# Fourier mixing and a gated MLP on one core: the transform along D as seven products in the stream of the sequence transform, the result transposed, and the gate computed from padded columns of w1

## The chip, the cores and the metric

The kernel runs on one core of a Trainium2 chip. The metric is device time in microseconds (us): the median of three runs of the kernel before is 736.44 us (736.27 to 736.62). Times of single instructions come from one profiled execution.

## What is computed

The input `x` is one sequence of S = 2048 rows with D = 512 columns, in float32. Two branches are computed from it and mixed by a gate:

```python
g = sigmoid((x * gate_w).sum(-1, keepdims=True))       # one number for each row
a = x @ Wd_re.T;  b = x @ Wd_im.T                      # transform along D
A = Ws_re @ a - Ws_im @ b                              # transform along S, 2048 x 2048 matrices
B = (silu(x @ w1) * (x @ w3)) @ w2                     # F = 1376 inner columns
out = g * A + (1 - g) * B
```

The kernel takes the transform along S first, on `x`, and the one along D after it, which gives the same `A`.

## The kernel before, in words

**Numbers.** Every float32 operand of a product is split into a high part (ScalarE, `split`, line 77) and a low part (VectorE, line 78), and every product of two tiles is three products on TensorE (`mm3`, line 82): high by high, high by low, low by high. A product here means one instruction with a 128 x 128 stationary tile and 512 moving columns. A 2 x 2 block product is done with seven block products instead of eight, from sums of the blocks ("forms").

**Stages, in the order of TensorE.**

1. *Gate and up, first half* (`gate_up(1, NC)`): the 1376 columns of w1 and w3 are padded to 11 units of 128 (NC = 11). Unit `i` makes `silu(x w1) * (x w3)` for 1024 rows of x. Its weights are loaded (`load_w`), split into `wa{i}` (`prep_wa`, three units ahead) and, after four sums on VectorE (`wu{i}`), into `wb{i}` (`prep_wb`, one unit ahead). `first1` and `first2` make two of the seven products three units ahead; `second` makes the other five and the tile `h{i}`. VectorE adds results in PSUM (lines 184, 201, 203), ScalarE applies Silu.
2. *Down, first half* (`down(0, ...)`): 11 groups of 24 products accumulate h @ w2 for those rows in all eight PSUM banks. Group `c` needs the splits `ho{i}` and `w2o{i}` of unit i (`prep_dn`), made one group ahead in two buffers each. Between groups stand pieces of other work (`extra`): the loads and splits of x for the second half, and `load_score`, which multiplies x by `gate_w` and sums along a row. At the end the eight banks are copied out and stored to DRAM (`bsp`).
3. *Gate and up, second half* (units 11 to 21), and
4. *Down, second half* (`down(1, ...)`, units 11 to 21): here the extra pieces are `load_a(p)`, p = 0 to 7, which loads a piece `xr{p}` of x and makes the forms of x as the stationary operands `a1_p` and `a2_p`, and the first steps of the next stage.
5. *Sequence transform* (`fourier_step`, lines 503 to 549): four blocks of 7 forms (P1, P5, P6, P3, P7, P2, P4) x 4 steps of 12 products. The moving operands are the blocks of the transform matrices (`cc`), loaded on SP five steps ahead (`advance`), summed into forms on VectorE (`sum_c`, line 462), split three steps ahead into one of four `zo` buffers (`split_c`), and for T3 changed in place by an accumulating DMA from POOL's queue (line 473). Results are combined on ScalarE and VectorE and stored to DRAM as `zsp`.
6. *Transform along D* (`dft_hid`): 384 products read `zsp` back through `load_z`; each result tile of 128 rows is scaled by the gate, a number for each partition, and added to the scaled `bsp` tile (lines 606 and 608), then stored.

**What sets the order.** The tile framework orders the instructions of each engine when the program is built, and every engine runs its own list strictly in that order, SP's and POOL's DMA issues too. The 13 buffers `f4` (128 x 1024 float32) serve all loads, the `h` tiles and the staging; a load is issued when its buffer is free.

Of the kernel before, what the change touches and what calls it, by code (L numbers as in the profile page):

```python
# [28 lines left out]
def fnet_swiglu_gate_kernel(  # L29
# [3 lines left out]
    xs: bass.AP,  # L33
# [5 lines left out]
    gw: bass.AP,  # L39
    out: bass.AP,  # L40
):

# [42 lines left out]
    gw_sb = const.tile([P, D], F32, tag="gw", name="gw_sb")  # L85
    score = const.tile([P, NST], F32, tag="score", name="score")
    gate_t = const.tile([P, NST], F32, tag="gate_t", name="gate_t")
    ngate_t = const.tile([P, NST], F32, tag="ngate_t", name="ngate_t")
    bsp = dram.tile([S, D], F32, tag="bsp", name="bsp")
    zsp = dram.tile([4 * NTB * P, 1024], F32, tag="zsp", name="zsp")  # L90

# [87 lines left out]
    def first2(i):  # L179

        y = bank(4 + i % 2, f"Y{i}")
        prod(y, i, 1, 1, True)
        s1 = G[i][1]
        nc.vector.tensor_add(s1, s1, y)
        nc.scalar.activation(s1, s1, AF.Silu)

    def second(i, between):
# [18 lines left out]
        prod(x, i, 6, 2, False, True)  # L206
        nc.scalar.activation(g1, x, AF.Silu)
# [18 lines left out]
    def down(g, extra):  # L226
        e = g * NC + NC - 1
        late = [6 + (e + 1) % 2, 6 + e % 2, e % 4]
        order = [k for k in (4, 5, 0, 1, 2, 3) if k not in late] + late
        acc = [bank(k, f"acc{g}_{k}") for k in order]  # L230
        for c in range(NC):
            if c + 1 < NC:
                prep_dn(g * NC + c + 1)
            h, w = HO.pop(g * NC + c), W2O.pop(g * NC + c)
            for i in range(2 * NT):
                sl = slice(i * P, (i + 1) * P)
                mm3(acc[i], h[:, 0, sl], h[:, 1, sl], w[:, 0], w[:, 1], c == 0, c == NC - 1)
            if c in extra:
                extra[c]()
        for i in range(NT):  # L240
            o = wide(f"b{g}_{i}")
            nc.scalar.activation(o[:, :512], acc[2 * i], AF.Copy)
            nc.vector.tensor_copy(o[:, 512:], acc[2 * i + 1])
            r0 = (2 * g * NT + 2 * i) * P
            nc.sync.dma_start(bsp[r0 : r0 + 2 * P, :].rearrange("(a p) d -> p a d", a=2),
                              o.rearrange("p (a d) -> p a d", a=2))
        return order

    def gate_up(i0, i1):
        for i in range(i0, i1):  # L250
# [10 lines left out]
            def b1(i=i):  # L261
                if i + LOOK < i1:
                    first2(i + LOOK)

# [9 lines left out]
    nc.scalar.activation(score[:, :1], warm[:, :1], AF.Silu)  # L274
# [47 lines left out]
    nc.sync.dma_start(gw_sb, gw.to_broadcast([P, D]))  # L322
# [60 lines left out]
    def load_score(p):  # L383
        r, t = wide(f"sr{p}"), wide(f"st{p}")
        nc.sync.dma_start(r, xs[p])
        for j in range(2):
            u = 2 * p + j
            sl = slice(j * 512, (j + 1) * 512)
            nc.vector.scalar_tensor_tensor(t[:, sl], r[:, sl], 1.0, gw_sb, op0=ALU.mult,
                                           op1=ALU.mult, accum_out=score[:, u : u + 1])  # L390

# [3 lines left out]
    for p in range(NG):  # L395
        extra.setdefault(1 + p, []).append(lambda p=p: load_score(p))
# [15 lines left out]
    def flat(ap):  # L412
        return ap.rearrange("p a n -> p (a n)")

    def load_a(p):

        r = wide(f"xr{p}").rearrange("p (a n) -> p a n", a=4)
        m = wide(f"xm{p}").rearrange("p (a n) -> p a n", a=4)  # L420
        nc.sync.dma_start(flat(r), xn[p])
        a21, a11, a12, a22 = (r[:, i] for i in range(4))
        nc.vector.tensor_sub(m[:, 0], a22, a21)
        for d, v, w in ((1, m[:, 0], a11), (2, a12, m[:, 1])):
            nc.vector.scalar_tensor_tensor(m[:, d], v, -1.0, w, op0=ALU.mult, op1=ALU.subtract)
        nc.vector.tensor_sub(m[:, 3], a11, a21)
        split(A1[p][:, 0, 0], A1[p][:, 1, 0], a11)
        split(flat(A1[p][:, 0, 1:4]), flat(A1[p][:, 1, 1:4]), flat(m[:, 0:3]))
        split(flat(A2[p][:, 0, 0:2]), flat(A2[p][:, 1, 0:2]), flat(r[:, 2:4]))
        split(A2[p][:, 0, 2], A2[p][:, 1, 2], m[:, 3])  # L430
# [6 lines left out]
    NQ = NG // 2  # L437
    NJ = len(CHAIN) * NQ
    NSTEP = NTB * NJ
# [5 lines left out]
    LOADS = sorted((tb * NJ + n + q, tb, k, q)  # L445
                   for tb in range(NTB) for q in range(NQ)
                   for k, n in ((0, 0), (1, NQ - 1), (2, 2 * NQ - 1), (3, 5 * NQ)))

    def step_of(m):
        tb, r = divmod(m, NJ)  # L450
        j, q = divmod(r, NQ)
        return tb, q, *CHAIN[j]

    def sum_c(m):

        if not 0 <= m < NSTEP:
            return
        tb, q, k, form = step_of(m)
        b = {"T1": "B11", "T2": "B22", "T4": "B21"}.get(form)
        if b:  # L460
            t = RAW[tb, "B12", q]
            nc.vector.tensor_add(t, t, RAW[tb, b, q])  # L462

    def split_c(m):

        if not 0 <= m < NSTEP:
            return
        tb, q, k, form = step_of(m)
        src = RAW[tb, {"T1": "B12", "T2": "B12", "T4": "B12", "T3": "B22"}.get(form, form), q]
        t = ZO[m] = zo.tile([P, 2, 1024], F32R, tag="zo", name=f"zo{m}")  # L470
        split(t[:, 0], t[:, 1], src)
        if form == "B22":
            nc.gpsimd.dma_start(src, cc[tb, 1, q], accum_op=ALU.add)

    def advance(m):
        while LOADS and LOADS[0][0] <= m + LEAD + AHEAD:
            _, tb, k, q = LOADS.pop(0)
            r = RAW[tb, BLOCKS[k], q] = wide(f"c{k}_{tb}_{q}")
            nc.sync.dma_start(r, cc[tb, k, q])
# [4 lines left out]
    for p in range(NG):  # L484
        xacts[p].append(lambda p=p: load_a(p))
    xacts[7].append(lambda: advance(-4))
# [5 lines left out]
    nc.scalar.activation(gate_t, score, AF.Sigmoid)  # L492
    nc.vector.tensor_scalar(ngate_t, gate_t, -1.0, 1.0, op0=ALU.mult, op1=ALU.add)
    advance(-1)

    def spill(tb, k, t):
        nc.sync.dma_start(zsp[(tb * 4 + k) * P : (tb * 4 + k + 1) * P, :], flat(t))
# [5 lines left out]
    def fourier_step(m):  # L503
        tb, q, k, form = step_of(m)
        if q == 0 and k in ("P1", "P5", "P2"):
            banks = {"P1": XB[tb % 2], "P5": ZB, "P2": YB}[k]
            U[k] = [bank(b, f"{k}_{tb}_{r}") for r, b in enumerate(banks)]
        ps = U[{"P6": "P1", "P7": "P1", "P4": "P1", "P3": "P5"}.get(k, k)]
        z = ZO.pop(m)
        own = k in ("P1", "P5", "P2")  # L510
        for i in range(2):
            w = (A1 if k in ("P1", "P5", "P6", "P3") else A2)[2 * q + i]
            b = slice(i * 512, (i + 1) * 512)
            for r in range(2):
                sl = slice(r * P, (r + 1) * P)
                mm3(ps[r], w[:, 0, FORM[k], sl], w[:, 1, FORM[k], sl], z[:, 0, b], z[:, 1, b],
                    own and q == 0 and i == 0, q == NQ - 1 and i == 1, not own)
        advance(m)
        if q < NQ - 1:
            return  # L520

        def out(name):
            U[name] = ut.tile([P, 2, 512], F32, tag=name, name=f"z{name}_{tb}")
# [7 lines left out]
        if k == "P1":  # L531
            out("s1")
        elif k == "P5":
            out("p5")
        elif k == "P6":
            out("u2")
        elif k == "P3":
            plus("u2")
            spill(tb, 2, U["u2"])
        elif k == "P7":  # L540
            out("u3")
            nc.vector.tensor_add(flat(U["p5"]), flat(U["p5"]), flat(U["u3"]))
            spill(tb, 3, U["p5"])
        elif k == "P2":
            plus("s1")
            spill(tb, 0, U["s1"])
        else:
            out("c21")
            spill(tb, 1, U["c21"])


    DW, ZY = [], {}

    def load_d(q):
        r = wide(f"dr{q}")
        nc.sync.dma_start(r, dd[q])
        t = yd.tile([P, 2, 1024], F32R, tag=f"d{q}", name=f"d{q}")
        split(t[:, 0], t[:, 1], r)
        DW.append(t)

    def load_z(m):
        if m >= 4 * NTB:
            return
        r = wide(f"zr{m}")
        nc.sync.dma_start(r, zsp[m * P : (m + 1) * P, :])
        t = yz.tile([P, 2, 1024], F32R, tag="zy", name=f"zy{m}")
        split(t[:, 0], t[:, 1], r)
        ZY[m] = t

    N1 = NSTEP - 3 * NQ  # L570
    for n in range(N1):
        fourier_step(n)
    close(a1_cm)
    yd_cm, yd = pool("yd", 1, "left")
    yz_cm, yz = pool("yz", 4, "left")
    for n in range(N1, NSTEP):
        fourier_step(n)
        k = n - N1
        if k < 4:
            load_d(k)  # L580
        elif k < 8:
            load_z(k - 4)

    def cols(n):
        if n < NST - 1:
            return ((slice(0, D), nc.scalar),)
        return ((slice(0, D // 2), nc.scalar), (slice(D // 2, D), nc.sync))

    def dft_hid(tb):
        ks = (XB[0], ZB) if tb % 2 == 0 else (YB, XB[1])  # L590
        acc = [bank(k, f"y{tb}_{i}") for i, k in enumerate((*ks[0], *ks[1]))]
        for q in range(4):
            z, w = ZY.pop(tb * 4 + q), DW[q]
            for i in range(NT):
                for j in range(2):
                    sl = slice(j * 512 + i * P, j * 512 + (i + 1) * P)
                    b = slice(j * 512, (j + 1) * 512)
                    mm3(acc[i], z[:, 0, sl], z[:, 1, sl], w[:, 0, b], w[:, 1, b],
                        q == 0 and j == 0, q == 3 and j == 1)
            load_z(tb * 4 + q + 4)  # L600
        for i in range(NT):
            n = tb * NT + i
            t = ut.tile([P, 2, 512], F32, tag=("s1", "p5", "u2", "u3")[i], name=f"o{n}")
            b, o = t[:, 0], t[:, 1]
            nc.sync.dma_start(b, bsp[n * P : (n + 1) * P, :])
# [66 lines left out]
```

## Time and profile before

| | |
|---|---|
| median of the runs | 736.44 us |
| the profiled execution | 736.15 us, of which the span of instructions is 734.4 us |
| TensorE products / weight loads | 728.6 us busy, 3196 / 598.6 us |
| VectorE | 499.5 us busy, 645 instructions |
| ScalarE | 347.6 us busy, 455 instructions |
| GpSimd (POOL) | 14.3 us busy, 20 instructions |
| moved by DMA | 104.09 MB, mean 142 GB/s |

How to read it: the span is the time from the first to the last instruction of the profiled execution. A row of the chain of work is start, length and what. A row of the timeline is start, length, engine, line, operation, output<-inputs, shape, and in brackets the idle time before it with what ended it; neighbours of one kind are merged as "x2". A row of a group ends with the count, the busy time, the mean ns of one, the idle time before them and what ended it. A row of a DMA group has its count, its size and the median time from issue to landing. L82 is line 82 of the kernel.

### The profile page before, as it was taken

The numbers are of one execution on the slowest core, as the hardware profiler recorded it, in microseconds if no ns is written. First come the engines' busy times: TensorE is split into PE (matmuls) and PEld (weight loads), VectorE is DVE, ScalarE is ACT, GpSimd is POOL, SyncE is SP. The second block draws the span as 40 slices with busy tenths as digits, with TensorE's granted clock in tenths as the row PEclk, the third lists the DMA queues.
The fourth block names the chain that finished last, engine by engine and source line by source line (L and its number), as shares of the span: only waits on it lengthen the run. The fifth ranks groups of instructions, "written<-read, shape, count | busy, mean of one in ns | idle before, by whom it ended". The sixth has DMA issues, their size and how long they took to land.

```text
span 734.4 us, 8387 instructions
## 1 busy us (share of the span) xinstructions
PE 728.6 (99%) x3196; PEld 598.6 (82%) x3196; DVE 499.5 (68%) x645; ACT 347.6 (47%) x455; POOL 14.3 (2%) x20
## 2 busy tenths in 40 slices
PE   9999999999999999999999999999999999999997
PEld 5788888888888888888888888888888888888886
DVE  6997788793687768996857585758575858514331
ACT  6755553454554444763544454445444447323330
POOL 0000000000000000000010001000100010000000
PEclk9999999999999999999999999999999999999999
DMA  7112117533013002656297608770677159833331
GB/s 271 55 62 86 58 59 254 174 129 116 30 57 115 1 29 79 213 211 258 114 211 246 230 1 172 250 249 17 131 247 247 64 98 318 288 127 116 116 114 58
DMA packets 33464, 104.09 MB, mean 142 GB/s; under 512 B 3600, under 2 KB 3984, under 8 KB 33424
## 3 DMA queue, kind: packets, MB, share of 16 engines
q1 hardware_dynamic: 28816, 91.11, 35.4%
q0 software_dynamic: 2304, 8.39, 6.3%
q10 hardware_dynamic: 2304, 4.06, 1.5%
q8 instruction: 25, 0.41, 0.2%
q14 instruction: 15, 0.12, 0.1%
HBM read 86.77 MB, written 16.78 MB: 141 GB/s over the span
## 4 chain that ended last, share of the span: by engine, by line
PE 98%; DMA 1%; DVE 0%; SPq 0%; ACT 0%; DVEq 0%; issue 0%
PE P L82 41%; PE acc L82 16%; PE X L82 16%; PE y L82 12%; PE Z L82 8%; PE Y L82 4%; PE C L82 1%; DMA xs<-xt 1%; DVE xo L78 0%; ACT xo L77 0%; DVE o L608 0%; SPq L101 0%; DVEq L668 0%; SPq L132 0%; DVEq L608 0%
## 5 line engine op out<-in xcount | busy, mean ns | idle before, releaser
L82 PE MATMUL P<-zo,a 128*128 128x512 f32 x1344 | 304.9, 389 | 0.0
L82 PEld LDWEIGHTS P<-zo,a 128*128 128x128 f32 x1344 | 252.3, 188 | 52.4
L78 DVE TENSOR_TENSOR zo<-c,zo 128x1024 fp32r<-128x1024 f32 x112 | 137.1, 1225 | 80.5 <-ACT zo L77 79.8
L77 ACT ACTIVATE zo<-c 128x1024 fp32r<-128x1024 f32 x112 | 118.4, 1058 | 131.2 <-PE P L82 123.0
L82 PE MATMUL acc<-w2o,ho 128*128 128x512 f32 x528 | 120.1, 389 | 0.0
L82 PEld LDWEIGHTS acc<-w2o,ho 128*128 128x128 f32 x528 | 99.1, 188 | 20.7
L82 PE MATMUL X<-xo,wb 128*128 128x512 f32 x378 | 93.8, 390 | 0.0
L82 PE MATMUL y<-d,zy 128*128 128x512 f32 x384 | 87.2, 389 | 0.0
L82 PEld LDWEIGHTS y<-d,zy 128*128 128x128 f32 x384 | 72.1, 188 | 15.0
L82 PEld LDWEIGHTS X<-xo,wb 128*128 128x128 f32 x378 | 70.6, 188 | 15.6 <-DVE u L201 0.5
L462 DVE TENSOR_TENSOR c<-c,c 128x1024 f32<-128x1024 f32 x48 | 58.6, 1226 | 8.9 <-DMA c<-cc 7.7
L78 DVE TENSOR_TENSOR zy<-zr,zy 128x1024 fp32r<-128x1024 f32 x16 | 19.5, 1224 | 49.9 <-ACT zy L77 49.9
L77 ACT ACTIVATE zy<-zr 128x1024 fp32r<-128x1024 f32 x16 | 16.9, 1058 | 40.8 <-PE y L82 39.9
L77 ACT ACTIVATE wa<-ws 128x768 fp32r<-128x768 f32 (+2 forms) x23 | 18.8, 819 | 33.2 <-PE Z L82 32.0
L82 PE MATMUL X<-xo,wa 128*128 128x512 f32 x126 | 32.7, 391 | 0.0
L82 PE MATMUL Y<-xo,wa 128*128 128x512 f32 x126 | 32.5, 389 | 0.0
L82 PE MATMUL Z<-xo,wb 128*128 128x512 f32 x126 | 32.3, 389 | 0.0
L82 PE MATMUL Z<-xo,wa 128*128 128x512 f32 x126 | 32.2, 389 | 0.0
L78 DVE TENSOR_TENSOR wb<-wu,wb 128x1024 fp32r<-128x1024 f32 x21 | 25.7, 1225 | 8.2 <-ACT wb L77 8.1
L78 DVE TENSOR_TENSOR ho<-h,ho 128x1024 fp32r<-128x1024 f32 x22 | 27.0, 1225 | 2.4 <-ACT ho L77 2.4
L82 PEld LDWEIGHTS X<-xo,wa 128*128 128x128 f32 x126 | 23.4, 188 | 5.5 <-DVE wa L78 0.6
L82 PEld LDWEIGHTS Y<-xo,wa 128*128 128x128 f32 x126 | 23.7, 188 | 4.9
(78 smaller groups left out, 553.8 us busy)
## 6 DMA issues: line engine op xcount, KB each, us to landing
c<-cc SPq DMA_DIRECT2D x64, 512.0 KB, 4.6
ws<-w SPq DMA_DIRECT2D x21, 512.0 KB, 3.2
c<-cc POOLq DMA_DIRECT2D x16, 512.0 KB, 5.3
zr<-zsp SPq DMA_DIRECT2D x16, 512.0 KB, 5.6
w2r<-w SPq DMA_DIRECT2D x10, 512.0 KB, 3.5
xs<-xt SPq DMA_DIRECT2D x16, 256.0 KB, 5.1
sr<-xs SPq DMA_DIRECT2D x8, 512.0 KB, 4.1
bsp<-b SPq DMA_DIRECT2D x8, 512.0 KB, 3.0
```

Source lines behind the costliest of these rows:

```text
L77: nc.scalar.activation(hi, src, AF.Copy)
L78: nc.vector.tensor_sub(lo, src, hi.bitcast(F32))
L82: nc.tensor.matmul(ps, u, v, start=first and n == 0, stop=last and n == 2, skip_group_check=chain)
L462: nc.vector.tensor_add(t, t, RAW[tb, b, q])
```

## The change

- *The transform along D* joins the stream of the sequence transform as blocks 4 and 5 of 7 forms x 2 steps. The stationary operands are now the forms of D's matrices and the moving ones are blocks of `zsp`, so the result comes out transposed, D x S, and the kernel's output is transposed on the host. `dft_hid`, `load_d` and `load_z` leave.
- *D's forms* are made by `prep_d`, one piece in each of units 12 to 15, with `forms`, the code that `load_a` also uses. They lie in the two `ho` buffers until they are stored to DRAM (`dsp`), and are loaded as `D1` and `D2` during the last 12 steps of block 3.
- *The down stages* swap stationary and moving operand, so their results are transposed too. They are scaled by 1 - g at once, by a row tile `NG_T`, and stored as `nbsp`.
- *The gate* comes from the 32 padded columns of w1, which now hold `gate_w`: unit 10 (and 21) computes the score for each row of x on the way. `put_score` copies it out and stores it as `gs`; `gates(g)` loads it as a row for all 128 partitions, takes the sigmoid, makes 1 - g on VectorE, negates half of g and stores the tile (`gsp`), which is loaded again as `GT` before block 4. `load_score` and its loads leave.
- *The end*: in blocks 4 and 5 a result is multiplied by the gate on VectorE, `nbsp` is added to it by an accumulating DMA on POOL's queue, and SP stores it. The last result adds `nbsp` on VectorE instead.

```diff
+    def forms(r, m, t1, t2):
...
+        nc.vector.tensor_sub(m[:, 0], a22, a21)
+        for d, v, w in ((1, m[:, 0], a11), (2, a12, m[:, 1])):
+            nc.vector.scalar_tensor_tensor(m[:, d], v, -1.0, w, op0=ALU.mult, op1=ALU.subtract)
+        nc.vector.tensor_sub(m[:, 3], a11, a21)
+        split(t1[:, 0, 0], t1[:, 1, 0], a11)
+        split(flat(t1[:, 0, 1:4]), flat(t1[:, 1, 1:4]), flat(m[:, 0:3]))
+        split(flat(t2[:, 0, 0:2]), flat(t2[:, 1, 0:2]), flat(r[:, 2:4]))
+        split(t2[:, 0, 2], t2[:, 1, 2], m[:, 3])
+
+    def prep_d(p):
+        r, m = wide(f"dr{p}"), wide(f"dm{p}")
+        t1 = dn.tile([P, 2, 4, 256], F32R, tag="ho", name=f"d1_{p}")
+        t2 = dn.tile([P, 2, 4, 256], F32R, tag="ho", name=f"d2_{p}")[:, :, :3]
+        nc.sync.dma_start(r, dd[p])
+        forms(r, m, t1, t2)
+        nc.sync.dma_start(dsp[0][p], t1.bitcast(F32))
+        nc.sync.dma_start(dsp[1][p], t2.bitcast(F32))
...
+    def put_score(i, j, gate):
+        if i % NC < NC - 1:
+            return
+        if j == 0:
+            SC[i] = tp.tile([P, 2, 512], F32, tag="sc", name=f"sc{i}", bufs=1)
+        nc.scalar.activation(SC[i][F % P :, j], gate[F % P :], AF.Copy)
+        if j == 1:
+            nc.sync.dma_start(gs[2 * (i // NC) : 2 * (i // NC) + 2].rearrange("b o n -> o b n"),
+                              SC[i][F % P : F % P + 1])
...
             for i in range(2 * NT):
-                sl = slice(i * P, (i + 1) * P)
-                mm3(acc[i], h[:, 0, sl], h[:, 1, sl], w[:, 0], w[:, 1], c == 0, c == NC - 1)
+                sl = slice(i // 2 * P, (i // 2 + 1) * P)
+                b = slice(i % 2 * 512, (i % 2 + 1) * 512)
+                mm3(acc[i], w[:, 0, sl], w[:, 1, sl], h[:, 0, b], h[:, 1, b],
+                    c == 0, c == NC - 1)
...
             o = wide(f"b{g}_{i}")
-            nc.scalar.activation(o[:, :512], acc[2 * i], AF.Copy)
-            nc.vector.tensor_copy(o[:, 512:], acc[2 * i + 1])
...
+            nc.vector.tensor_mul(o[:, :512], acc[2 * i], NG_T[g][:, :512])
+            nc.scalar.activation(o[:, 512:], acc[2 * i + 1], AF.Copy)
+            nc.vector.tensor_mul(o[:, 512:], o[:, 512:], NG_T[g][:, 512:])
+            nc.sync.dma_start(nbsp[i * P : (i + 1) * P, g * 1024 : (g + 1) * 1024], o)
...
+    def gates(g):
+        t, NG_T[g] = wide(f"gt{g}"), wide(f"ng{g}")
+        nc.sync.dma_start(t.rearrange("p (b n) -> p b n", b=2),
+                          gs[2 * g : 2 * g + 2].rearrange("b o n -> o b n").to_broadcast([P, 2, 512]))
+        nc.scalar.activation(t, t, AF.Sigmoid)
+        nc.vector.tensor_scalar(NG_T[g], t, -1.0, 1.0, op0=ALU.mult, op1=ALU.add)
+        nc.scalar.activation(t[:, 512:], t[:, 512:], AF.Copy, scale=-1.0)
+        nc.sync.dma_start(gsp[g], t)
...
             def b1(i=i):
                 if i + LOOK < i1:
                     first2(i + LOOK)
+                if 0 < i - NC <= KD:
+                    prep_d(i - NC - 1)
...
-    for p in range(NG):
-        extra.setdefault(1 + p, []).append(lambda p=p: load_score(p))
+    extra.setdefault(2, []).append(lambda: gates(0))
...
+    NQ = [NG // 2] * NTB + [KD // 2] * (NTB // 2)
+    STEPS = [(blk, q, k, form) for blk, nq in enumerate(NQ) for k, form in CHAIN for q in range(nq)]
+    START = [sum(NQ[:blk]) * len(CHAIN) for blk in range(len(NQ) + 1)]
...
+    def block(blk, k, q):
+        if blk < NTB:
+            return cc[blk, k, q]
+        return z_rows(2 * (blk - NTB) + (0, 1, 1, 0)[k], (0, 0, 2, 2)[k] + q)
...
+    xacts[2].append(lambda: gates(1))
...
+    def spill(blk, k, t, ps=None):
+        last = blk == len(NQ) - 1 and k == 1
+        if blk < NTB:
...
+            return nc.sync.dma_start(z_rows(blk, k), flat(t))
...
+        for r in range(2):
+            nc.vector.tensor_mul(t[:, r], t[:, r] if ps is None else ps[r], gt)
+            if last:
+                nc.vector.tensor_add(t[:, r], t[:, r], b[:, r])
+                (nc.scalar if r else nc.sync).dma_start(o[:, r], t[:, r])
+        if not last:
+            nc.gpsimd.dma_start(t, nb, accum_op=ALU.add)
+            nc.sync.dma_start(o, t)
...
+    for n in range(N1, len(STEPS)):
+        k = n - N1
+        if k < 2 * KD:
+            nc.sync.dma_start((D1 + D2)[k].bitcast(F32), dsp[k // KD][k % KD])
+        elif k < 2 * KD + 2:
+            nc.sync.dma_start(GT[k - 2 * KD], gsp[k - 2 * KD])
+        step(n)
...
-    for tb in range(NTB):
-        dft_hid(tb)
...
+    w13[0, :, F:] = a["gate_w"][:, None]
```

212 lines of the change are left out of this document (77 added, 135 removed).

## The prediction

> **What bounds the kernel now.** I read the page's busy shares and its chain of work first, then the chain in order of time.
>
> ```profile
> span 734.4 us, 8387 instructions
> ...
> PE 728.6 (99%) x3196; PEld 598.6 (82%) x3196; DVE 499.5 (68%) x645; ACT 347.6 (47%) x455; POOL 14.3 (2%) x20
> ...
> PE 98%; DMA 1%; DVE 0%; SPq 0%; ACT 0%; DVEq 0%; issue 0%
> ```
> ```profile
> 113.95 59.88 PE acc L82 x264
> ...
> 278.72 59.88 PE acc L82 x264
> 338.60 304.69 PE P L82 x1344
> 643.29 87.05 PE y L82 x384
> 730.34 0.04 DVEq L608
> ```
>
> TensorE is the chain, and in the rows of the chain (start, length, what) each piece begins where the one before ends, up to 730.34 us: no gaps. So removed products are worth their full time, and everything else costs nothing until it makes TensorE wait. A product takes 87.05 / 384 = 0.2267 us. After the last one the span goes on for 734.4 - 730.34 = 4.06 us: the last arithmetic and the last store.
>
> ```profile
> 8.00:12.00 4.00, 4.00 (x19) 3.25 (x18) 3.62 (x7) 3.24 (x7) 0.00 (x0) 1.00 1.03 399
> ```
> ```profile
> 181.00:278.70 97.70, 97.70 (x432) 80.73 (x431) 68.15 (x104) 45.93 (x70) 0.00 (x0) 1.00 0.12 44
> 278.72:338.60 59.88, 59.88 (x265) 49.57 (x265) 55.63 (x95) 37.13 (x59) 0.00 (x0) 1.00 0.49 169
> 338.60:643.29 304.69, 304.69 (x1346) 252.26 (x1345) 206.88 (x181) 144.76 (x159) 14.06 (x16) 1.00 0.61 187
> ```
>
> These windows (columns PE, PEld, DVE, ACT, POOL, granted clock, DMA share, GB/s) give the cover. The clock is full, DMA reaches 399 GB/s where it is loaded. VectorE is the engine to watch: 55.63 of 59.88 us (93%) in the second down stage, 68.15 of 97.70 (70%) in the gate and up products before it, 68% in the sequence transform.
>
> **Products removed: -10.9 us.** The old D transform takes 384 products. The new blocks 4 and 5 take 2 blocks x 7 forms x 2 steps x 12 = 336. 48 x 0.2267 = 10.9 us. The down stages only swap the stationary and the moving operand, both 128 wide and 512 long as before; the count stays at 528.
>
> By the Trainium skill, "TensorE: Matmul & The Clock Gate", Back-to-back issue gap, products with 512 columns follow each other at about 131 ns; then 48 of them would be worth an estimated 6.3 us. The trace disagrees with 227 ns and decides.
>
> **VectorE's spacing.** A queue is walked with start-to-start times, which the timeline of a packed stretch gives:
>
> ```profile
> 302.67 1.23 DVE L78 TENSOR_TENSOR ho<-h,ho 128x1024 fp32r<-128x1024 f32 x1
> ...
> 319.00 1.24 DVE L78 TENSOR_TENSOR ho<-h,ho 128x1024 fp32r<-128x1024 f32 x1
> 320.13 0.97 DVE L78 TENSOR_TENSOR a<-xm,a 128x768 fp32r<-128x768 f32 x1
> 321.00 0.70 DVE L78 TENSOR_TENSOR a<-xr,a 128x512 fp32r<-128x512 f32 x1
> 321.61 0.44 DVE L78 TENSOR_TENSOR a<-xm,a 128x256 fp32r<-128x256 f32 x1
> 321.94 2.38 DVE L78 TENSOR_TENSOR zo<-c,zo 128x1024 fp32r<-128x1024 f32 x2
> ...
> 330.49 0.71 DVE L78 TENSOR_TENSOR w2o<-w2r,w2o 128x512 fp32r<-128x512 f32 x1
> ```
>
> 1024 columns take 1.13 us to the next start, 768 take 0.87, 512 take 0.61, 256 take 0.33. One preparation of a form tile (`forms`: four operations on 256, then splits of 256, 768, 512, 256) takes 5 x 0.33 + 0.87 + 0.61 + 0.33 = 3.46 us.
>
> **First down stage: 0.**
>
> ```profile
> 115.06 0.68 DVE L208 TENSOR_TENSOR h<-g,u 128x512 f32<-128x512 f32 x1
> ```
> ```profile
> L389 DVE SCALAR_TENSOR_TENSOR st<-sr,gw_sb 128x512 f32<-128x512 f32 x16 | 10.6, 689 | 2.2 <-DMA sr<-xs 2.2
> ```
>
> `load_score` leaves, 10.6 us of VectorE that lay under products, and `gates(0)` comes: a table load, a sigmoid, one VectorE operation. The row's load is issued when `wu13` is done, about 119.0 by the order after 115.06 (one split, four sums, two issues on SP). ScalarE then stops for it, and behind it wait `w2o3` and `ho3`. `ho3`'s low half is wanted at 113.95 + 3 x 5.44 + 0.2 = 130.5 us and ends 4.1 us after the load has landed (sigmoid 1.06, then 1.13 + 0.61 + 1.13 and signals), so the load may take 7.4 us. `put_score`'s two copies of 0.6 us delay only the last `h`, which is wanted nine groups later.
>
> **Gate and up, second half: +0.9 us.**
>
> ```profile
> L78 DVE TENSOR_TENSOR wb<-wu,wb 128x1024 fp32r<-128x1024 f32 x21 | 25.7, 1225 | 8.2 <-ACT wb L77 8.1
> ...
> L201 DVE TENSOR_TENSOR u<-u,X 128x512 f32<-128x512 f32 x21 | 14.4, 685 | 16.6 <-PE X L82 16.4
> ...
> L149 DVE TENSOR_TENSOR wu<-ws 128x256 f32<-128x256 f32 x21 | 8.9, 424 | 0.5
> ```
>
> `prep_d` puts one form preparation into each of four units. A unit lasts 42 products or 9.52 us and holds 0.87 + 1.13 + 4 x 0.33 + 5 x 0.61 = 6.4 us of VectorE by spacing; with 3.46 that is 9.8, 0.3 too much, 1.2 us in four units, which the lead of the splits takes up. Walking the printed order of the changed program, the four units still meet TensorE, but the splits `ho11` and `ho12`, which stand early now, have moved behind (D's tiles hold their buffers until stored), and the low half of `wb18` comes 0.9 us late. Bounds: 0, and 7.8 if every instruction held VectorE for its full duration (7.3 + 4.2 - 9.52 = 2.0, four times).
>
> **Second down stage: +3.0 us.** Here the cover is thin. In the printed order VectorE and ScalarE come to the gate row after `load_a(2)`. The row's load reuses the buffer of `xr1`, so it is issued at about 289.5; with 5.2 us or less it is there when ScalarE arrives.
>
> ```profile
> 290.74 2.40 SPq L421 DMA_DIRECT2D xr<-xn  x2
> ```
> ```profile
> 288.76 0.69 DVE L78 TENSOR_TENSOR a<-xr,a 128x512 fp32r<-128x512 f32 x1
> ```
> ```profile
> 293.49 1.19 ACT L77 ACTIVATE a<-xm 128x256 fp32r<-128x256 f32 x2 [1.34 <-DVE xm L426]
> ```
> ```profile
> L492 ACT ACT_TABLE_LOAD x1 | 1.3, 1283 | 0.0
> L77 ACT ACTIVATE zo<-c 128x1024 fp32r<-128x1024 f32 x112 | 118.4, 1058 | 131.2 <-PE P L82 123.0 <-issue 4.9 <-DMA c<-cc 1.7
> ```
> ```profile
> xr<-xn SPq DMA_DIRECT2D x8, 512.0 KB, 3.7
> ```
>
> ScalarE: 294.7 + 1.28 (table) + 1.06 (sigmoid) = 297.0; VectorE's complement (1.13) to 298.2; ScalarE's negated half (0.6) to 298.9. Only then does SP issue the store of the gate tile, and behind it in SP's queue stands the load of `xr3`, which today goes out at 290.74. It is issued at 299.6 and lands 3.7 later, with up to 1.3 more for the store's bytes ahead of it; I take 303.7. Until then VectorE does `ho15`, `w2o15`, `w2o16` and `ho16`, which ends at 303.4 (today 303.9, with `load_a(3)` already behind it). From 303.7 the order up to the last split of weights, `w2o21`, is 5 preparations (17.3), 5 `ho` (5.65), 5 `w2o` (3.05), 4 `zo` (4.5) and 2 sums (2.26): 32.8 us, so 336.5 plus 0.1 for the signal. TensorE wants `w2o21`'s low half at 338.60 - 24 x 0.2267 + 2 x 0.2267 = 333.6. It waits 3.0 us. Today `w2o21` ends at 331.2, so the 2.4 us of slack are what the first lateness eats. Bounds: 0, if the walk is late by its own error, and 8.6 with full durations (38.4 instead of 32.8 us).
>
> The scaled copies at the stage's end (8 VectorE operations for 4) free the first transform's banks first; I take 0.
>
> **The D stream's own waits: 0.** D's form tiles are written out (7 MB) and read back during the last 12 steps of block 3, 32.7 us; at 399 GB/s they need 18. In each new block VectorE has 20 operations on 1024 columns, 1 add of 1024 and 12 of 512: 31 us by spacing in 14 steps of 2.72, 38.1 us. The tightest wait is the accumulate that turns B22 into T3: two steps lie between the two, not four.
>
> ```profile
> c<-cc POOLq DMA_DIRECT2D x16, 512.0 KB, 5.3
> ...
> bsp<-b SPq DMA_DIRECT2D x8, 512.0 KB, 3.0
> ...
> zsp<-zu SPq DMA_DIRECT2D x4, 512.0 KB, 5.0
> ...
> gw_sb<-gw SPq DMA_DIRECT2D x1, 256.0 KB, 7.2
> ...
> out<-o SPq DMA_DIRECT2D x1, 128.0 KB, 1.7
> ```
>
> With 5.3 us block 5's T3 is ready about 1 us before it is wanted. Bounds 0 and 1. In SP's printed order every load of block 5 and the last load of `nbsp` stand ahead of the first output store, so stores that wait for an accumulate hold no load; behind the store of `zs1` of block 4 waits only a ScalarE read with a lead of three steps.
>
> **The tail: +3.2 us.**
>
> ```profile
> 731.33 0.34 SPq L610 DMA_DIRECT2D out<-o  x1
> ```
> ```profile
> DMA to landing us min/median/max: 5.1/5.3/6.7
> ```
>
> P2 of block 5 ends 2 steps, 5.44 us, before the end. VectorE adds and scales it in 4 x 0.61 plus 0.2, done 2.8 us before the end; the accumulate takes 5.3, SP issues the store 2.5 us after the end (0.33), it lands 3.0 later, and the last result's store goes beside it. Today the last store lands at 731.33 + 1.7 and the span ends 1.4 later; 2.5 + 0.3 + 3.0 + 1.4 = 7.2 against 4.06. Bounds: +0.9 (an accumulate as fast as a store, 3.0) and +6.6 (the slowest accumulate, 6.7, and a store of 5.0).
>
> By the Trainium skill, "DMA: Bandwidth & Descriptors", Anatomy of one DMA, a GpSimd DMA takes about 2.0 us and its bytes at 436 GB/s, an estimated 3.2 us for 512 KB; the tail would be 2.1 us shorter and the sum -5.9. The sixteen accumulates of the trace took 5.3.
>
> **Sum.** -10.9 + 0.9 + 3.0 + 3.2 = -3.8 us. The profiled execution took 736.15 us (span 734.4); the median of the runs is 736.44, 0.3 more. Forecast 736.15 - 3.8 = 732.4 us.
>
> **Rivals.**
> 1. *The cover holds.* VectorE's two lags stay inside the slack. For it: 2.4 us of slack now, and no TensorE wait today. Against: a fixed order that is 5 us later. 736.15 - 10.9 + 3.2 = 728.5.
> 2. *VectorE becomes the bound at full durations.* Each operation starts only when the one before has ended, as where it needs its result. 7.8 in gate and up, 8.6 in the second down stage: 736.15 - 10.9 + 7.8 + 8.6 + 3.2 = 744.9. It decides from a surplus of 10.9 - 3.2 = 7.7 us in both. Against it: the spacings above.
>  The Trainium skill, "VectorE: DVE Perf Modes", The DRAIN you can't avoid, says that the next operation does not start until the pipeline is empty, and speaks for this rival; the starts at 319.00 and 320.13 under a duration of 1.24 speak against it here.
> 3. *The gate row's broadcast load is the wait.* 128 partitions read one row. `gw_sb`, half as large, took 7.2 us; twice that, 14.4, exceeds the cover by 7.0 in the first and 9.2 in the second down stage: 732.4 + 16.2 = 748.6, and slower than before from 8.3 us on. Against: `gw_sb` stood in a queue that moved 399 GB/s, at the end of it.
>
> That the products stay is excluded: the printed program has 336.
>
> **How the numbers follow.** Forecast 0.45 (its own range 730 to 735), rival 1 0.25, rival 2 0.21, rival 3 0.09. A measurement of this kernel tells 0.2%, 1.5 us, from no change. Faster: 0.40 + 0.25 = 0.65; within: 0.05 of the forecast and 0.03 of rival 2, 0.08; slower 0.27. The range 728 to 740 leaves out rival 3, the upper part of rival 2 and a little below.
>
> **What would show it.** Blocks 4 and 5 as 336 products of 0.227 us; a TensorE wait of about 3 us for `w2o` near 334 us and about 1 us for `wb` before; `xr3` landing near 304; the span ending about 7 us after the last product, with an output store as the last landing. No wait at `w2o`, or one before `ho3` or `ho15`, makes the forecast wrong.

## The result and the profile after

| | before | after |
|---|---|---|
| median of the runs | 736.36 us (4 runs, 736.08 to 736.62) | 745.25 us (4 runs, 745.09 to 745.51) |
| ratio | | 1.0121, 95% interval 1.0104 to 1.0139 |
| profiled execution, its span | 736.15, 734.4 us | 745.09, 743.2 us |

The forecast was 732.4 us, with 728 to 740: the change costs 8.9 us where 4 were to be won. The page of the changed kernel, its busy shares and its chain of work:

```profile
span 743.2 us, 8371 instructions
...
PE 719.9 (97%) x3148; PEld 588.8 (79%) x3148; DVE 537.3 (72%) x685; ACT 368.8 (50%) x487; POOL 26.2 (4%) x31
...
PE 78%; issue 9%; DVE 6%; DMA 3%; ACT 1%; POOL 1%; SPq 0%; POOLq 0%; DVEq 0%; ACTq 0%
```

TensorE has 48 products less and is busy 8.7 us less, but it is 78% of the chain and not 98%. The timeline of TensorE (start, length, line, output<-inputs, number, and the wait before) has the stretches one after the other:

```profile
279.59 56.18 PE L81 MATMUL acc<-ho,w2o 128*128 128x512 f32 x245
337.48 4.61 PE L81 MATMUL acc<-ho,w2o 128*128 128x512 f32 x19 [1.70 <-DVE w2o L77]
341.92 304.81 PE L81 MATMUL P<-zo,a 128*128 128x512 f32 x1344
646.57 49.12 PE L81 MATMUL P<-zo,d 128*128 128x512 f32 x216
698.59 11.17 PE L81 MATMUL P<-zo,d 128*128 128x512 f32 x48 [2.89 <-ACT zs L589]
710.95 0.50 PE L81 MATMUL P<-zo,d 128*128 128x512 f32 x1 [1.19 <-ACT zu L589]
711.73 16.43 PE L81 MATMUL P<-zo,d 128*128 128x512 f32 x71 [0.27 <-DVE zo L77]
```

The sequence transform is as long as before. Block 4 (the first 168 of the `zo,d` products) runs through. Block 5 stops TensorE three times, for 4.4 us in all. The last product ends at 711.73 + 16.43 = 728.16, and the span goes on for 15.0 us after it, the tail. The timeline of POOL shows what it does in that time (L558 is the addition of `nbsp`, L510 the one that makes T3):

```profile
674.66 1.22 POOL L558 DMA_DIRECT2D zu<-nbsp  x1 [12.94 <-DVE zu L553]
681.18 1.21 POOL L558 DMA_DIRECT2D zp<-nbsp  x1 [5.29 <-DVE zo L77]
688.30 1.21 POOL L558 DMA_DIRECT2D zs<-nbsp  x1 [5.91 <-DVE c L499]
695.29 1.21 POOL L558 DMA_DIRECT2D zc<-nbsp  x1 [5.78 <-issue]
703.94 0.91 POOL L510 DMA_DIRECT2D c<-zsp  x1 [7.45 <-DVE zo L77]
705.17 0.87 POOL L510 DMA_DIRECT2D c<-zsp  x1 [0.33 <-issue]
718.09 1.20 POOL L558 DMA_DIRECT2D zu<-nbsp  x1 [12.05 <-DVE zu L553]
724.56 1.22 POOL L558 DMA_DIRECT2D zp<-nbsp  x1 [5.27 <-DVE zs L593]
731.84 1.20 POOL L558 DMA_DIRECT2D zs<-nbsp  x1 [6.06 <-issue]
```

Two additions of `nbsp` never stand closer than 6.5 us, whatever their data do, while the two T3 accumulates at 703.94 and 705.17 follow each other at once. "issue" as the releaser says that POOL waited for nothing that the profile shows. By the lines of L558, an addition takes this long from issue to landing:

```profile
DMA to landing us min/median/max: 6.2/6.8/7.0
```

And the waits of the last 97 us (who waited for whom, us in total, times, longest):

```profile
DVE zo L77 <- ACT zo L76: 23.5, 8, 7.3
ACT zo L76 <- DMA c<-zsp: 13.9, 4, 6.5
ACT zs L589 <- DMA out<-zs: 8.9, 1, 8.9
...
PE P L81 <- ACT zs L589: 2.9, 1, 2.9
```

ScalarE stops four times for T3 and once, for 8.9 us, before it may read block 5's P1 into the tile `zs`, since block 4's result in that tile is still to be stored. All these stops hold up the splits behind them.

### The profile page after: what moved, and what is told of

It is laid out like the page before. It is cut to its first block, busy times and chain, and to the rows that moved or that the text cites. A ratio compares the mean times of both kernels' runs of the same rounds, so it can differ in the third digit from the quotient of the medians.

```text
span 743.2 us, 8371 instructions
## 1 busy us (share of the span) xinstructions
PE 719.9 (97%) x3148; PEld 588.8 (79%) x3148; DVE 537.3 (72%) x685; ACT 368.8 (50%) x487; POOL 26.2 (4%) x31
## 3 DMA queue, kind: packets, MB, share of 16 engines
q0 software_dynamic: 4784, 14.16, 10.9%
## 4 chain that ended last, share of the span: by engine, by line
PE 78%; issue 9%; DVE 6%; DMA 3%; ACT 1%; POOL 1%; SPq 0%; POOLq 0%; DVEq 0%; ACTq 0%
PE P L81 38%; PE X L81 15%; PE acc L81 12%; PE Z L81 8%; PE Y L81 4%; DMA c<-zsp 3%; DVE a L77 1%; PE C L81 1%; DVE zo L77 1%; DMA xs<-xt 1%; DVE xm L102 0%; DVE ho L77 0%; DVE w2o L77 0%; DVE c L499 0%; SPq L625 0%
## 5 line engine op out<-in xcount | busy, mean ns | idle before, releaser
L77 DVE TENSOR_TENSOR zo<-c,zo 128x1024 fp32r<-128x1024 f32 x140 | 170.7, 1223 | 111.8 <-ACT zo L76 111.3
L76 ACT ACTIVATE zo<-c 128x1024 fp32r<-128x1024 f32 x140 | 147.4, 1059 | 168.8 <-PE P L81 136.8
L81 PE MATMUL acc<-ho,w2o 128*128 128x512 f32 x528 | 120.7, 390 | 1.8 <-DVE w2o L77 1.7
L81 PEld LDWEIGHTS acc<-ho,w2o 128*128 128x128 f32 x528 | 98.9, 188 | 23.3 <-DVE w2o L77 2.7
L81 PE MATMUL P<-zo,d 128*128 128x512 f32 x336 | 77.2, 390 | 4.4 <-ACT zs L589 2.9
L499 DVE TENSOR_TENSOR c<-c,c 128x1024 f32<-128x1024 f32 x60 | 73.2, 1223 | 8.1 <-DMA c<-cc 5.9
L81 PEld LDWEIGHTS P<-zo,d 128*128 128x128 f32 x336 | 62.9, 188 | 18.5 <-ACT zs L589 3.3
L510 POOL DMA_DIRECT2D c<-cc x16 | 14.0, 876 | 592.9 <-DVE zo L77 592.9
L81 PEld LDWEIGHTS Z<-xo,wb 128*128 128x128 f32 x126 | 23.7, 188 | 5.0
```

The source lines that it names most:

```text
L76: nc.scalar.activation(hi, src, AF.Copy)
L77: nc.vector.tensor_sub(lo, src, hi.bitcast(F32))
L81: nc.tensor.matmul(ps, u, v, start=first and n == 0, stop=last and n == 2, skip_group_check=chain)
L499: nc.vector.tensor_add(t, t, RAW[blk, b, q])
L510: nc.gpsimd.dma_start(src, block(blk, 1, q), accum_op=ALU.add)
```

## The experiments

Theory **Q**: the additions of `nbsp` are let in one at a time on GpSimd's queue, about 7 us apart; that makes block 4's store of `zs` late and with it ScalarE and TensorE, and it makes the tail long. Rivals: **B**, the single `zs` buffer alone; **L**, the 7 MB of form tiles read back at block 4's start; **W**, formed after the first runs, the stop for T3, which in these short blocks stands only two steps behind B22; **V**, no room on VectorE. Ratios are against the kernel before, with their 95% intervals; the changed kernel has 1.0121.

### 1 to 4: the additions, the buffer, the rows, the descriptors

```diff
 # e1_vector_add: as the last result has it, for all eight
+            nc.vector.tensor_add(t[:, r], t[:, r], b[:, r])     # b: loaded by SP at P1 and P3 of the block
-            nc.gpsimd.dma_start(t, nb, accum_op=ALU.add)
 # e2_two_zs
-            U[name] = ut.tile([P, 2, 512], F32, tag=name, name=f"z{name}_{blk}")
+            U[name] = ut.tile([P, 2, 512], F32, tag=name, name=f"z{name}_{blk}", bufs=2 if name == "s1" else 1)
 # e3_rows_4k
-    nbsp = dram.tile([D, S], F32, tag="nbsp", name="nbsp")
+    nbsp = dram.tile([NTB, 2, P, 2, 512], F32, tag="nbsp", name="nbsp")
 # e4_ring_2k
-    nc = bacc.Bacc("TRN2", target_bir_lowering=False, num_devices=1, dynamic_dma_scratch_size=1024)
+    nc = bacc.Bacc("TRN2", target_bir_lowering=False, num_devices=1, dynamic_dma_scratch_size=2048)
```

> All eight results of blocks 4 and 5 get their nbsp part as the last one does: a load by SP, some steps ahead, and two VectorE additions; GpSimd accumulates only the four T3 tiles. Theory Q (the nbsp accumulates admit each other only about 7 us apart on GpSimd's queue, so the store of zs of block 4 is late, the next block's read of P1 into that tile waits 8.9 us, and the tail is long): the TensorE waits of 2.9 and 1.2 us in block 5 go, the products end near 342.1 + 304.5 + 76.2 = 722.8, the span about 5.9 us later as the last result's own additions and store took in the changed kernel; span 728.7, time 730.6. Rival L (the 7 MB of form tiles read back delay block 4's and 5's own loads): the TensorE waits stay, products end at 728.2, time about 736. Rival V (VectorE has no room for sixteen more additions of 0.61 us): waits for zo in both blocks, time 733 or more.

> The tile zs of the blocks' first result gets a second buffer; everything else as in the changed kernel, the accumulates too. Theory Q: ScalarE's read in block 5 no longer waits 8.9 us and TensorE's 2.9 us go, but the accumulates still stand 7 us apart; T3 of block 5 may have to wait for zc of block 4 (3.5 us of TensorE) or not; the last store of zs lands at 733 to 736; time 735.5 to 739. Rival B (the single buffer is the whole cause, the queue's spacing costs nothing by itself): products end at 722.8, zs is done at 719.8 and its accumulate starts at once, 6.8 + 2.8 + 1.4 later the span ends; time near 732.5. Rival L (loads of the form tiles): no change, 745.

> The scratch nbsp is laid out so that each accumulate reads one run of 4 KB per partition (128 rows) in place of two of 2 KB (256 rows); the same bytes, the same queue, the same tiles. Theory Q with its cause in the number of rows (two accumulates of 128 rows were admitted 1.2 us apart at 703.94 and 705.17, never two of 256): the issues of block 4 follow the data (zp near 679.7, zs near 683.3), each lands about 5.3 us after its issue, no TensorE wait in block 5, time near 732. Rival S (GpSimd's accumulates are always one after the other, whatever their rows): issues 5.6 us apart, zs of block 4 issued near 685.9; time near 734. Rival L: no change, 745.

> Only the scratch memory for GpSimd's DMA descriptors is doubled, from 1024 to 2048 bytes per partition; the program is the same. Theory Q with its cause in room for descriptors: two accumulates of 256 rows stand in the queue at once, issues follow the data, each still lands about 6.8 us after its issue; zs of block 4 is stored by 693.5, TensorE does not wait in block 5, products end at 722.8, zs of block 5 lands near 726.6, time near 733. Rival S (one accumulate after the other for another reason): issues stay 6.5 to 7.1 us apart, time 745.

| | median us | ratio |
|---|---|---|
| e1_vector_add | 737.82 | 1.0016 (1.0007 to 1.0026) |
| e2_two_zs | 744.49 | 1.0114 (1.0095 to 1.0133) |
| e3_rows_4k | 739.60 | 1.0038 (1.0023 to 1.0053) |
| e4_ring_2k | 740.29 | 1.0053 (1.0037 to 1.0070) |

**The queue.** With twice the descriptor memory, and nothing else changed, POOL's additions of block 4 follow VectorE's results:

```profile
674.85 1.20 POOL L558 DMA_DIRECT2D zu<-nbsp  x1 [13.17 <-DVE zu L553]
680.47 1.20 POOL L558 DMA_DIRECT2D zp<-nbsp  x1 [4.42 <-DVE zp L553]
684.13 1.21 POOL L558 DMA_DIRECT2D zs<-nbsp  x1 [2.46 <-DVE zs L553]
687.37 1.21 POOL L558 DMA_DIRECT2D zc<-nbsp  x1 [2.04 <-DVE zc L553]
```

With half the rows for each DMA and the old memory it is the same:

```profile
681.71 0.87 POOL L559 DMA_DIRECT2D zp<-nbsp  x1 [4.64 <-DVE zp L554]
685.46 0.86 POOL L559 DMA_DIRECT2D zs<-nbsp  x1 [2.88 <-PE P L81]
688.72 0.86 POOL L559 DMA_DIRECT2D zc<-nbsp  x1 [2.39 <-DVE zc L554]
```

So what holds a DMA back is room for descriptors, counted in rows; rival S (additions always one after the other) is out. The Trainium skill, "DMA: Bandwidth & Descriptors", SWDGE vs HWDGE vs iDMA, says that GpSimd writes its descriptors into rings that lie in SBUF, and that only one queue is allocated to it. That a full ring holds up whatever comes next is read from these two runs.

**But neither run reached its 732 to 733.** Products still end at 728.7 and 727.6, since ScalarE still waits for the store of `zs`, here in e4:

```profile
ACT zs L589 <- DMA out<-zs: 7.9, 1, 7.9
```

Two or three additions now share the DMA engines with the stores. `zs` is issued at 684.13 and not at 688.30, its store on SP at 690.68 and not at 695.00, but ScalarE's read starts at 697.24 and not at 697.94: from the issue of the store to the read it was 2.9 us, and now it is 6.6, with the addition of `zc` under way beside it (that overlap is read from the times; it was not tried apart). What went is tail: 10.5 us instead of 15.0 (e4). Q has the tail right and is not the only cause of the stops.

**The buffer.** In e2 the stop for `zs` is gone, the products end 1.5 us sooner (726.7), and the rest stays. Both B (732.5) and Q (735.5 to 739) are wrong about its time. POOL shows what is next:

```profile
696.57 1.21 POOL L558 DMA_DIRECT2D zc<-nbsp  x1 [6.11 <-DVE c L499]
697.31 1.41 POOL L510 DMA_DIRECT2D c<-zsp  x1
704.00 0.87 POOL L510 DMA_DIRECT2D c<-zsp  x1 [5.28 <-issue]
```

T3 of block 5 comes in behind `zc`, its second half only when `zc` has landed; ScalarE waits for it, VectorE 8.4 us for ScalarE, and `zu`, whose work stands behind T3's split on both engines, is added at 716.89 against 718.09.

**VectorE additions.** e1 has no addition on POOL at all and still loses, in block 4 and 5:

```profile
DVE zo L77 <- ACT zo L76: 17.6, 9, 6.9
ACT zo L76 <- DMA c<-zsp: 12.3, 4, 7.3
...
PEld P L81 <- DVE zo L77: 5.9, 6, 1.6
```

ScalarE stops 7.3 us for T3, VectorE behind it 6.9 us. With 36 us of work in the 38 us of a block VectorE can't make that up. Q's 730.6 is out. V's "733 or more" holds, but V has no reason for the stop ahead of it. L's marks are nearly met: it set the end of the products at 728.2 and the time at about 736, and they came to 728.4 and 737.8; e6 decides on L. The stop for T3 is W, and the next runs try it.

### 5 to 8: no addition, another order, straight into out, the early stages

```diff
 # e5_no_nbsp
-            nc.gpsimd.dma_start(t, nb, accum_op=ALU.add)
 # e6_p2_before_p7: P2 between P3 and P7, in blocks 4 and 5 only
+    LATE7 = tuple(CHAIN[n] for n in (0, 1, 2, 3, 5, 4, 6))
 # e7_into_out: down() stores o into out, and
-            nc.gpsimd.dma_start(t, nb, accum_op=ALU.add)
-            nc.sync.dma_start(o, t)
+            nc.gpsimd.dma_start(o, t, accum_op=ALU.add)
 # e8_early_stages
-        nc.sync.dma_start(gsp[g], t)
+        nc.scalar.dma_start(gsp[g], t)
-        nc.scalar.activation(SC[i][F % P :, j], gate[F % P :], AF.Copy)      # put_score
+        nc.scalar.activation(o[:n], gate[:n], AF.Silu)                       # n = 96; the row is stored from o
```

> Leaves out the addition of nbsp to seven of the eight results of blocks 4 and 5: no accumulate stands between the scaling and the store. Theory A (the accumulates are the whole loss: their spacing, their traffic and the stores behind them): no TensorE wait in blocks 4 and 5, products end near 722.8, the span 5.9 later; time 730.6. Theory W (T3 stands only two steps behind B22 here, so ScalarE and then VectorE stop about 7 us for its accumulate in each block, and VectorE, which has 31 us of work in 38, comes late with the splits): TensorE waits of 1 to 3 us for zo near P7 of block 5 stay, products end at 724 to 726, time 732 to 734.

> In blocks 4 and 5 the products run P1, P5, P6, P3, P2, P7, P4: two more steps between B22 and T3. The accumulates of nbsp stay as they are. Theory W: ScalarE's waits for T3 (6.5 us in each block of the changed kernel) fall below 2, VectorE's idle 4 to 7 us before them go, and no TensorE wait is left in block 5; products end near 722.8. Then the accumulates, 7 us apart, set the end: zu lands at 716, zs at 723, zp at 730, its store 4.2 before the end; time 736.4. Theory A alone: T3 of block 5 still stands in GpSimd's queue behind zc of block 4 until 702, TensorE waits 2 us or more, products end at 725 or later, time 739 or more.

> The down stages store their part straight into out, and seven of the eight results of blocks 4 and 5 are accumulated into out by one GpSimd DMA from their tile; the load into the tile and the store behind it go. Same rows of 2 KB, so by theory Q the accumulates stay about 7 us apart; a tile is free 3 us sooner, TensorE's 2.9 us in block 5 shrink to 0 to 1, and the store of 2.8 us behind the last accumulate goes: time 739 to 740. Rival H (adding in the chip's memory costs more than adding in the tile, as the destination must be read there): 9 us or more for each, time 745 or more.

> Two edits before the sequence transform: the gate tile is stored from ScalarE's queue, so that SP's load of xr3 does not stand behind it, and the score row is stored from the tile it is in (Silu takes only the 96 partitions that hold columns of w1), so that the 0.63 us copy ahead of the first Silu goes. If SP's block is what costs the second down stage its 2.4 us, xr3 lands near 296, TensorE does not wait for w2o, the down stage takes 59.9 us again, the first one starts at 113.95, the transform at 339.0, and everything behind comes 3.0 us sooner: 742.2. Rival V (VectorE has too much work in that stage, 63 us by durations, whatever the loads do): the down stage still takes 61 us or more, 743.5 or more.

| | median us | ratio |
|---|---|---|
| e5_no_nbsp | 732.98 | 0.9950 (0.9930 to 0.9970) |
| e6_p2_before_p7 | 736.27 | 0.9997 (0.9988 to 1.0007) |
| e7_into_out | 736.00 | 0.9994 (0.9985 to 1.0004) |
| e8_early_stages | 745.84 | 1.0125 (1.0108 to 1.0142) |

**e5** leaves out seven of the eight additions, so its output is not the layer's. Its median lies where W put it (732 to 734) and not where A (the additions are the whole loss) did, 730.6. But the trace doesn't show what W said of it, waits of 1 to 3 us in block 5:

```profile
649.36 25.36 PE L81 MATMUL P<-zo,d 128*128 128x512 f32 x109
675.48 51.75 PE L81 MATMUL P<-zo,d 128*128 128x512 f32 x227 [0.76 <-DVE zo L77]
```

ScalarE still stops for T3, for 7.2 us in block 4 and 5.5 in block 5, but TensorE only once, for 0.76 us in block 4. The two blocks take 77.9 us, 1.1 more than in e6 below. The trace puts no more than that on T3. The four runs lie between 730.84 and 734.72, and the profiled one, the longest, is late by 2.3 us where the first down stage begins, in a stage that the edit doesn't touch. The rows of the chain, the changed kernel's first:

```profile
114.56 59.88 PE acc L81 x264
```
```profile
116.84 59.88 PE acc L81 x264
```

So e5's time doesn't choose between A and W; its trace gives the stop for T3 about 1 us where no addition is in the way.

**e6** came out at 736.27 where W said 736.4. The timeline of TensorE and a row of the waits:

```profile
647.50 76.73 PE L81 MATMUL P<-zo,d 128*128 128x512 f32 x336
```
```profile
ACT zo L76 <- DMA c<-zsp: 2.2, 1, 2.2
```

All 336 products run without a stop, and ScalarE's waits for T3 fall from 13.9 to 2.2 us, though the form tiles are still read back at the same place: L is out, and so is A alone, which put 739 or more. The order moves `zs` from the third to the second place on POOL too, so this run alone doesn't separate W from B; e10 does. What is left is tail: the products end at 724.23, the span at 735.0, and the additions are still 6.2 to 7.1 us apart.

**e7** gained 3 us more than expected. One DMA takes the place of two, and by the lines of its L558 it is not slower but quicker than the addition in the tile:

```profile
DMA to landing us min/median/max: 5.9/6.0/6.2
```

That is against rival H (adding in the chip's memory costs more). The Trainium skill, "DMA: Bandwidth & Descriptors", Anatomy of one DMA, puts most of a DMA's fixed cost into the receipt of its last write and calls the chip's memory the heaviest target; the addition into it took 6.0 us here and the one into the tile 6.8, so no such price shows. Most of the difference may be the store that runs beside an addition into a tile: those of `zu`, which have none beside them, took 6.2 us in the changed kernel.

**e8** missed. The first stage's 0.5 us came back (its down stage starts at 114.10), but the second down stage took 61.9 us, 0.4 less, and TensorE still waited for `w2o`:

```profile
PE acc L81 <- DVE w2o L77: 1.5, 1, 1.5
```

`xr3` was issued at 293.35 and not at 299.99, and it helped little: SP's block is not what costs this stage. The transform started 0.9 us sooner, but blocks 4 and 5 took 1.8 us more than in the changed kernel, with a wait of 0.76 us in block 4 and 3.25 at `zs`; why is not settled.

### 9 to 12: the gate row, and the causes put together

```diff
 # e9_gate_row_late
-    xacts[2].append(lambda: gates(1))
+    xacts[10].append(lambda: gates(1))
 # e10_p2_first_vector_add = e6 + e1
 # e11_p2_first_into_out = e6 + e7
 # e12_all_mended = e6 + e7 + e4 + e8 + e9
```

> The gate row of the second half is loaded, and its sigmoid and complement are made, after the eleventh group of the second down stage in place of the third; SP's queue as in the changed kernel otherwise. Theory O (in the third group these operations push load_a(3) behind w2o16 and ho16, which wait for tiles that TensorE still reads, so VectorE idles some 5 us between 294 and 302 and has no room to catch up): TensorE no longer waits for w2o, the stage takes 59.9 to 60.4 us in place of 62.3, the transform starts near 339.9, time 743.0. Rival V (the stage has too much VectorE work wherever it stands): the wait for w2o stays at 2 us or more, time 745. Rival E (the late row delays the first splits of the transform instead): the stage takes 60, but TensorE waits 1 us or more for zo right behind it.

> P2 before P7 in blocks 4 and 5, as in the run before, and nbsp added by VectorE in all eight results, no GpSimd accumulate of nbsp. Theory W (what kept the version with VectorE additions at 737.8 was the stop for T3, 7 us in each block): with T3 four steps behind B22 no idle of VectorE over 3 us in the blocks, 36 us of its work fit into 38, TensorE waits under 1 us in all; products end near 724.2, the span 5.9 later; time 732. Rival V (no room on VectorE for 4.8 us more per block, whatever T3 does): TensorE waits of 2 us or more for zo, time 734.5 or more.

> P2 before P7 in blocks 4 and 5, and seven of the eight results accumulated straight into out. By theories W and Q together: no TensorE wait in the blocks (products end near 724.2), accumulates 6.3 us apart, zu at 710, zs at 716.3, zp at 722.6, landing at 728.8; the last result's own store ends 5.9 after the products, about 730; span 730.2, time 732.1. If only one of the two were the cause, no gain beyond the better of the two single runs: 736.

> P2 before P7 in blocks 4 and 5, results accumulated into out, twice the memory for GpSimd's descriptors, the gate row of the second half after the eleventh group and its gate tile stored from ScalarE's queue, the score row stored from the tile it is in. If the terms add up: 2.3 us from the second down stage, 0.5 from the first gate and up stage, none lost in blocks 4 and 5, so the products end near 721.4; the last result's arithmetic and store set the end 5.9 later; span 727.3, time 729.2. If the accumulates still set the end (zp issued by its data near 718, 6.2 to 8.5 to landing under the traffic of the others): span 727 to 728.5, time 729 to 730.5. If the late gate row costs at the transform's start: 731 or more.

| | median us | ratio |
|---|---|---|
| e9_gate_row_late | 742.83 | 1.0085 (1.0069 to 1.0102) |
| e10_p2_first_vector_add | 731.18 | 0.9936 (0.9911 to 0.9960) |
| e11_p2_first_into_out | 732.96 | 0.9950 (0.9935 to 0.9965) |
| e12_all_mended | 728.79 | 0.9893 (0.9877 to 0.9910) |

**e9**: 743.0 was expected. The chain of e9 has the stage in one piece again:

```profile
280.14 59.88 PE acc L81 x264
340.02 9.99 PE P L81 x44
```

In the changed kernel the gate row stood in the third group. Three rows of VectorE's timeline there:

```profile
298.11 0.69 DVE L301 TENSOR_SCALAR ng<-gt 128x1024 f32<-128x1024 f32 x1 [1.15 <-ACT gt L300]
...
302.26 0.69 DVE L77 TENSOR_TENSOR w2o<-w2r,w2o 128x512 fp32r<-128x512 f32 x1 [1.37 <-ACT w2o L76]
...
304.35 0.42 DVE L100 TENSOR_TENSOR xm<-xr 128x256 f32<-128x256 f32 x1
```

VectorE waits for the sigmoid, then for `w2o16`'s buffer, and `load_a(3)` comes only at 304.35, where it began at 296.45 before and filled such holes. The work is the same in the eleventh group, where it costs nothing. So it is the place (O), not the amount (V). The edit also takes SP's block on `xr3` away, which by e8 is worth 0.4 us alone.

**e10** separates W: between e1 and e10 only the order differs (and with it the step at which two loads of `nbsp` are issued), neither has an addition on POOL, and the time falls from 737.82 to 731.18. VectorE has the 36 us per block in both. The traces place 4.5 of the 6.6 us: 3.0 in TensorE's stretch of blocks 4 and 5 and 1.5 in the tail; the rest is not located. In the profile TensorE waits once for VectorE, 1.4 us (V put 2 or more, W less than 1), and the time lies 1 us below the forecast.

**e11**: 732.1 was expected. The two cures add: e6 and e7 alone give 736.27 and 736.00.

**e12**: 729.2 was expected. It is 1.07% faster than the kernel before. TensorE's timeline, and POOL's last rows:

```profile
339.10 304.81 PE L81 MATMUL P<-zo,a 128*128 128x512 f32 x1344
643.75 76.73 PE L81 MATMUL P<-zo,d 128*128 128x512 f32 x336
```
```profile
711.72 1.23 POOL L552 DMA_DIRECT2D out<-zs  x1 [4.21 <-DVE zs L547]
718.35 1.20 POOL L552 DMA_DIRECT2D out<-zp  x1 [5.40 <-DVE zp L547]
```

The last product ends at 720.48, 6.7 us before the span's end, and the last additions are released by their data.

## Why the prediction was wrong, step by step

Times of stretches are from the chains and TensorE's timelines, which set before's last stretch at 643.13 to 730.33.

| step | forecast us | measured us |
|---|---|---|
| products removed: 76.73 without a stop (e6) for 87.20 | -10.9 | -10.5 |
| first gate and up stage | 0 | +0.6 |
| first down stage (59.88 us) | 0 | 0 |
| gate and up, second half (105.32 for 104.88) | +0.9 | +0.4 |
| second down stage (62.32 for 59.88) | +3.0 | +2.4 |
| the D stream's own waits (81.59 for 76.73) | 0 | +4.9 |
| tail (15.04 for 4.07) | +3.2 | +11.0 |
| sum of the spans | -3.8 | +8.8 |

**Two steps failed, and one price is behind both.** "The D stream's own waits: 0" and "The tail: +3.2 us" price an addition of `nbsp` at 5.3 us, from sixteen accumulates of 128 rows, issued 2.5 us or more apart, none of which had to wait for another. Seven of the new ones have 256 rows, take 6.8, and have to wait for each other; the prediction walked SP's and VectorE's queues and not POOL's.

- *D stream.* "behind the store of `zs1` of block 4 waits only a ScalarE read with a lead of three steps": that is the place, and the lead was not enough. The queue made the addition 5 us late (data ready at 683.2, issued at 688.30) and the store with it, ScalarE stood 8.9 us, and all its splits with it. The "tightest wait", T3 two steps behind B22, was named too, with 1 us of slack at 5.3 us. T3 took 7.7 us from issue to landing in block 4, where the DMA engines were full (a share of 1.05 from 658 to 666 us), and what it stops is not only its own split but everything behind it on ScalarE and VectorE. What each is worth on TensorE is in the table below: without additions T3's two steps cost 1.1 us (e5 against e6), so the other 3.7 of the 4.9 us need the additions. With VectorE nearly full, the same two steps cost 3.0 us (e1 against e10).
- *Tail.* P2's result was ready at 725.8, as the walk said (2.8 us before the end, 2.3 by the trace). Its addition was issued 6.0 us later, landed 6.8 later, and SP stored it at 738.88. Of the 7.8 us that the forecast lacks 6.0 are the queue, 1.5 the longer addition. The upper bound, +6.6, had no wait on POOL in it.

| run | blocks 4 and 5 on TensorE, us | tail, us |
|---|---|---|
| the changed kernel | 81.6 | 15.0 |
| e5, no additions | 77.9 | 5.4 |
| e6, P2 before P7, additions as they were | 76.7 | 10.8 |
| e4, twice the descriptor memory | 81.1 | 10.5 |
| e7, added straight into out | 77.8 | 10.0 |
| e1, additions on VectorE | 81.5 | 6.6 |
| e10, the same with P2 before P7 | 78.4 | 5.1 |
| e12, all together | 76.7 | 6.7 |

**Right in size, wrong in cause: the second down stage.** TensorE waited for `w2o` as forecast, 2.4 us instead of 3.0, and `xr3` came near 304. But e8 takes SP's block away and gets 0.4 us back; e9 moves the gate row and gets all of it. The printed order had the cause in it: `load_a(3)` behind `w2o16` and `ho16`.

**A small one missed.** `put_score`'s copy was said to delay "only the last `h`". It stands ahead of the Silu and of the `u` copy that frees a PSUM bank, in the chain of the first gate and up stage:

```profile
92.14 0.70 DVE s L211
...
92.87 0.64 ACT sc L224
...
95.72 0.49 ACT u L238
...
96.26 1.65 PE X L81 x6
```

**Right:** the worth of the products, the first down stage, no gain or loss in the sequence transform, the form tiles' traffic hidden, and the rejection of rivals 2 and 3: VectorE was no bound by itself, and the gate row's broadcast load took 4.2 us. That the result came out near rival 2's 744.9 is chance. The forecast also had no rival that begins at POOL, though the change puts seven DMAs in a row there.

## What to carry to other kernels

A price from a trace holds for the use it had there: before a DMA price is taken for a new place, compare the rows, and count how many stand in that queue at once. Walk every queue that gets new work, the DMA-issuing one that looks idle (POOL was 2% busy) before all. Where a stream's blocks get shorter, leads that are counted in steps of a block shrink with them, and an in-order engine that stops for one late tile stops for all behind it.

## What the runs showed of the hardware

- Room in GpSimd's DMA queue is counted in rows, not in bytes: every one of these DMAs moves 512 KB. The page of the changed kernel has 4784 packets on it:

```profile
q0 software_dynamic: 4784, 14.16, 10.9%
```

 Before, 16 accumulates of 128 rows made 2304, 144 each; the 20 of 128 rows now make 2880, so the seven of 256 rows have 272 each. With 1024 bytes of descriptor memory two of 144 went in at once, one of 272 and one of 144 too (696.57 and 697.31), but not two of 272, nor another 144 on top (704.00). With 2048 bytes two of 272 did.
- POOL is held 1.2 us by the issue of 256 rows and 0.87 by that of 128.
- An addition into the chip's memory took 5.9 to 6.2 us (e7), the same bytes into a tile 6.2 to 7.0 (the changed kernel), of which 6.2 where no store ran beside it.
- A store of 512 KB took 2.8 us beside one addition (the changed kernel) and 2.7 to 2.8 with none (e5), but up to 5.1 in e4, where two additions were under way together. That these are what slows it was not tried apart.
